# Two models in one kernel: x in eight chunks, the last weight rows loaded twice, and a new order of steps

## The chip, the cores and the metric

The kernel runs on one core of a Trainium2 chip. The metric is the device time of one execution in microseconds (us); less is better. TensorE (PE, with its weight loads PEld), VectorE (DVE), ScalarE (ACT), GpSimd (POOL) and SyncE (SP, which here only issues DMAs) each work through their own list of instructions strictly in order and wait for each other by semaphores.

## The reference, cut to what matters

Two independent models read a [2048, 448] input each and their outputs stand side by side in one [2048, 896] output. B, C and Lam are complex.

```
# A: 16 heads of 28, each token attends to 8 keys, 2 tokens apart
q, k, v = split(x_A @ wqkv)
logits[s, w] = q[s] . k[s - 2 w] * 28 ** -0.5        (w = 0..7, masked below token 0)
out_A = (softmax(logits) @ v[s - 2 w]) @ wo

# B: a diagonal state space model over the 2048 tokens
Bu = x_B @ (((Lam_bar - 1) / Lam) * B).T
h[t] = Lam_bar * h[t-1] + Bu[t]
out_B = 2 * real(h @ C.T) + x_B * Dskip
```

## The kernel before, in words

**Two tokens in one row.** x_A is read as [1024, 896]: a row holds an even token (columns 0 to 447) and the odd one behind it (448 to 895). For a product with the weights x has to stand with its columns on the partitions, so it is cut into chunks of 128 columns and each is transposed. With seven chunks (`xA`, [128, 7, 1024]) chunk 3 holds the even token's columns 384 to 447 on partitions 0 to 63 and the odd token's first 64 columns on partitions 64 to 127. The even token multiplies weight rows 0 to 447 as they come; the odd one needs the same rows shifted by 64 partitions. So `Wt` has seven chunks too, and six copies (`s1v`, `s2v`, `s1k`, `s2k`, `s1q` on DVE, `s2q` on ACT; lines 485 to 493) write the shifted weights on chip.

**The product.** `paired` (line 351) makes the steps of one product for 128 rows, which is 256 tokens: `e` are the three full matmuls of the even token, `o` those of the odd one, `f` both, `t` the two half-height matmuls on the last 64 weight rows. There are eight such products each of v, k and q (`v0` to `q7`, line 362 and 360 in the profile) and eight of the output projection (`w0` to `w7`). `ve`, `ke` and `qe` bring the sums from PSUM to SBUF; `kt` and `qt` then transpose the k and q rows by a transposed DMA into `Kt` and `Qt`. Four PSUM units are shared by number (the digit behind the engine letter in the list).

**How x gets there.** The first 512 rows (four tiles `xn`) come by plain loads and PE transposes them (`xt0a` to `xt3`, line 499, evacuated by `xe0a` to `xe3`). The last 512 rows come by transposed DMA straight from HBM: `xa2`, `xa3`, one DMA each (line 236). x_B comes by two transposed DMAs, `xb0` and `xb1`, of 512 rows each.

**Model B.** `nw` and `nt` load B into `natW` (`nt` are the four small loads of its last 64 rows), `lam0` to `lam6` mix them on DVE, `wtx0` to `wtx6` and `wr0` to `wr2` transpose the result by DMA into `WT`. `b30` to `b21` are the products with x_B (line 727; the second digit is the half of x_B, so `b11` is the first that reads what `xb1` brings), `ri`, `sc`, `ro` the scan on DVE. `ctn` and `ctl` load C and `c1m`, `c2m` mix it (line 540, with a first product `tc..` on POOL or ACT). `g0` to `g2` build a direct term. `y0` to `y7` are the output products (line 851 and 854); before a `y`, `xd` writes the skip term into PSUM from `xo`, which `xol` loads.

**Attention.** `s` are the logits of 128 rows, `x` the exponential on ACT, `a` the product with v, `n` the division on DVE, `ot` a transposed DMA, then the `w` products, `we` to SBUF and `wo` to HBM.

**The order.** Nothing is scheduled at run time. `ORDER` (line 27) is one list of steps, `name.engine` with the PSUM unit behind it, and each engine runs its steps in that order. All of SP's and ACT's DMAs run through eight semaphores, DMAHW0 to DMAHW7, handed out in turn: a DMA that takes a semaphore again is held on its issuing engine until the DMA that had it before has landed. POOL's DMAs have semaphores of their own (DMASW).

Of the kernel before, what the change touches and what calls it, by code (L numbers as in the profile page):

```python
# [32 lines left out]
lam1.V ve5.A0 q1t.P3 q1f.P3 tlam6.V qt0.S dia.G ve4.A1 td1.V k4f.P0 qe1.A3 xb0.S lam6.V k4t.P0 qe3.A2 td2.V v2t.P1
v6t.P3 tlam2.G v6f.P3 ke4.A0 p7.V v2o.P1 ve6.A3 v2e.P1 tlam4.G ts.A q6f.P2 wtx5.S q6t.P2 ctn.G k7t.P0 v7f.P3 ve2.V1
qe6.A2 wtx1.S v7t.P3 tb.V q5t.P2 ve7.A3 q5f.P2 kt3.S lam4.V tc.A cob.G b30.P1 qe5.V2 wtx0.S lam2.V s00.P be30.A1 qt1.S
k7f.P0 x00.A ri30.V wtx4.S b10.P1 sc300.V kt1.S ro30.V ke7.A0 ctl.S s01.P be10.A1 q4f.P0 x01.A ri10.V q4t.P0 k2t.P1
k2f.P1 qe4.A0 sc100.V s10.P qt2.S ke2.A1 b00.P0 sc101.V x10.A kt2.S ro10.V tc24.G kt7.S a00.P1 be00.A0 a01.P1 wtx6.S
s11.P tc23.G n0.V1 k5t.P0 x11.A k5f.P0 wtx2.S c24.V a10.P1 ri00.V tc21.G qt3.S ke5.A0 s20.P a11.P1 x20.A q7t.P0 xb1.S
q7f.P0 n1.V1 s21.P qe7.A0 c23.V k6f.P1 x21.A c21.V tc22.G k6t.P1 sc000.V a20.P0 qt4.S ke6.A1 s30.P sc001.V a21.P0
tc20.A kt6.S b20.P1 c22.V x30.A n2.V0 tc25.G kt4.S ro00.V kt5.S s31.P be20.A1 b11.P0 x31.A ot0.S c25.V ri20.V qt5.S  # L40
b31.P1 be11.A0 qt6.S c20.V sc200.V s40.P be31.A1 vg1.S b01.P0 tc12.A tc16.V qt7.S x40.A c16.V c12.V tc15.G ot1.S
sc201.V tc10.A s41.P be01.A0 c10.V a30.P1 a31.P1 c15.V tc14.A b21.P0 vg2.S n3.V1 x41.A tc11.G c14.V ot3.S kb.G c11.V
tc13.A s50.P ot2.S be21.A0 c13.V tc26.G a40.P1 ro20.V x50.A g1.P0 xol.G a41.P1 ge1.A0 s51.P ri11.V g0.P0 x51.A n4.V1
s80.P ge0.A0 c26.V ot4.S a50.P1 sc110.V x80.A a51.P1 wol.S g2.P0 n5.V1 gp2.A0 s60.P ge2.V0 x60.A a80.P1 ot5.S xd1.V0
n8.V1 y1.P0 sc111.V ot8.S xd0.V1 ro11.V s61.P y0.P1 x61.A ri21.V ye1.A0 yo1.S oc0.A a60.P0 sc210.V ye0.A1 yo0.S a61.P0
s70.P n6.V0 w3t.P1 x70.A w3f.P1 sc211.V ot6.S w0f.P0 we3.A1 wo3.S ro21.V w0t.P0 oc1.A s71.P we0.A0 wo0.S w4f.P1 x71.A
ri31.V w5f.P0 w5t.P0 w4t.P1 sc310.V w1t.P2 we4.A1 wo4.S w2t.P3 w1f.P2 we5.A0 wo5.S xd3.V1 w2f.P3 ro31.V we1.A2 wo1.S
# [930 lines left out]
```

## Time and profile before

| | us |
|---|---|
| time, median of 3 runs | 133.84 (133.19 to 134.24) |
| time of the profiled execution | 133.44 |
| span of its trace | 131.6 |
| PE busy | 123.5 (94% of the span) |
| DVE busy | 107.3 |
| ACT busy | 86.6 |
| POOL busy | 47.8 |
| granted PE clock | 0.995 |

The span is the stretch of the trace from the first to the last instruction; the time of the same execution is 1.84 us more. A row of the timeline gives start, duration, engine, line, operation and tiles. Rows with SPq, ACTq and POOL DMA are the issuing of a DMA and not the transfer; how long after the start of its issue a DMA has landed is listed apart. A row in the list of waits says who waited for whom: us in total, number of times, longest.

### The profile page before, as it was taken

How to read it: one execution, taken by the hardware profiler on the slowest of the kernel's cores; microseconds unless marked ns; L12 is line 12 of the kernel's file. 1: busy time of each engine (PE TensorE's matmuls, PEld its weight loads, DVE VectorE, ACT ScalarE, POOL GpSimd, SP SyncE). 2: the span in 40 equal slices, each digit the busy share in tenths (PEclk: the TensorE clock that was granted, in tenths of full speed). 3: DMA queues.
4: the chain of work that ended last, by engine and by line, in shares of the span. 5: the costliest groups of instructions: out<-in, count | busy, mean ns of one | idle time of the engine just before them, and what ended most of it. 6: DMA issues, size and time to landing. Idle time of an engine off the chain costs nothing.

```text
span 131.6 us, 3129 instructions
## 1 busy us (share of the span) xinstructions
PE 123.5 (94%) x1221; PEld 63.2 (48%) x1226; DVE 107.3 (81%) x225; ACT 86.6 (66%) x91; POOL 47.8 (36%) x75
## 2 busy tenths in 40 slices
PE   7899999999999999999999998799999999999960
PEld 2554444443444466544454656545644654445540
DVE  2569999998898999999999999999999999860000
ACT  3249779887999879968698957608797523222230
POOL 7998911899700946660077840000000000000000
PEclk9999999999999999999999999999999999999998
DMA  4999969799899995898979949890452652422222
GB/s 106 371 318 211 230 118 183 124 271 165 174 103 186 216 158 86 175 188 200 199 142 156 221 97 256 198 189 9 140 144 70 229 124 70 139 70 72 70 82 70
DMA packets 54546, 20.83 MB, mean 158 GB/s; under 512 B 46782, under 2 KB 54160, under 8 KB 54528
## 3 DMA queue, kind: packets, MB, share of 16 engines
q1 hardware_dynamic: 53376, 18.70, 69.4%
q0 software_dynamic: 656, 1.50, 4.0%
q10 hardware_dynamic: 496, 0.40, 0.9%
q8 instruction: 11, 0.18, 0.6%
q14 instruction: 7, 0.06, 0.2%
HBM read 5.30 MB, written 3.86 MB: 70 GB/s over the span
## 4 chain that ended last, share of the span: by engine, by line
PE 57%; DVE 29%; issue 4%; DMA 3%; POOL 2%; ACT 1%; SPq 0%; DVEq 0%
PE U L362 14%; PE U L851 11%; PE early L362 8%; PE late L851 4%; DVE rs L755 4%; PE U L854 3%; PE U L727 3%; DVE O L692 3%; PE U L360 3%; DVE natW L540 3%; DMA Wt<-in_A_wqkv_dram 3%; DVE C L540 3%; POOL wtmp L534 2%; DVE ra L742 2%; DVE rb L743 2%
## 5 line engine op out<-in xcount | busy, mean ns | idle before, releaser
L671 ACT ACTIVATE P<-s 128x1920 bf16<-128x1920 f32 (+1 forms) x16 | 28.6, 1786 | 5.7 <-PE s L649 5.6
L727 PE MATMUL U<-xB,WT 128*128 128x512 bf16 x93 | 22.1, 379 | 0.3
L362 PE MATMUL U<-Wt,xA 128*128 128x448 bf16 x90 | 19.7, 353 | 1.0 <-DVE Wt L339 0.5
L362 PEld LDWEIGHTS <-xA 128*128 128x128 bf16 x144 | 12.9, 98 | 15.1 <-issue 4.2
L534 POOL TENSOR_SCALAR wtmp<-CT,p_pah 128x448 f32<-128x448 bf16 x6 | 13.7, 2279 | 12.4 <-DVE rv L745 6.8
L335 ACT CAST ys<-U 128x896 bf16<-128x896 f32 (+1 forms) x11 | 9.5, 871 | 12.0 <-PE U L851 9.2
L851 PEld LDWEIGHTS <-h 128*128 128x128 bf16 x105 | 10.0, 98 | 9.2 <-DVE U L841 0.2
L727 PEld LDWEIGHTS <-WT 128*128 128x128 bf16 x98 | 9.2, 97 | 10.6
L362 PE MATMUL early<-Wt,xA 128*128 128x448 bf16 x54 | 11.7, 354 | 0.0
L335 ACT CAST u<-U 128x1024 bf16<-128x1024 f32 (+1 forms) x8 | 7.2, 905 | 4.5 <-PE U L727 4.4
L692 DVE TENSOR_TENSOR O<-U,rcs 128x896 bf16<-128x896 f32 (+1 forms) x9 | 9.8, 1090 | 0.3
L851 PE MATMUL U<-natW,h 128*128 128x448 bf16 x42 | 9.0, 353 | 0.1
L755 DVE TENSOR_TENSOR_SCAN rs<-p_r,ini,rv 128x512 bf16<-128x512 f32 x7 | 8.8, 1274 | 0.0
L680 PE MATMUL U<-Vt,P 128*128 128x29 bf16 x256 | 8.2, 176 | 0.6 <-DVE O L692 0.6
L755 DVE TENSOR_TENSOR_SCAN rs<-p_r,rv 128x512 bf16<-128x512 f32 x7 | 8.6, 1257 | 0.0
L680 PEld LDWEIGHTS <-P 128*128 128x128 bf16 x256 | 7.6, 96 | 2.1 <-issue 0.8
L335 ACT CAST ys<-late 128x896 bf16<-128x896 f32 (+2 forms) x6 | 4.3, 718 | 6.1 <-PE late L851 5.6
L362 PE MATMUL U<-wo,OT 128*128 128x448 bf16 x36 | 7.6, 353 | 0.0
L851 PE MATMUL U<-C,h 128*128 128x448 bf16 x35 | 7.4, 352 | 0.0
L335 ACT CAST Nx<-U 128x896 bf16<-128x896 f32 x7 | 6.4, 908 | 1.5 <-PE U L360 1.4
L534 POOL TENSOR_SCALAR wtmp<-CT,p_pag 128x448 f32<-128x448 bf16 x2 | 4.2, 2080 | 8.4 <-DVE C L540 8.4
L362 PEld LDWEIGHTS <-OT 128*128 128x128 bf16 x48 | 4.4, 98 | 4.9 <-issue 1.2
(198 smaller groups left out, 231.4 us busy)
## 6 DMA issues: line engine op xcount, KB each, us to landing
out_dram<-ys SPq DMA_DIRECT2D x15, 224.0 KB, 2.4
tmpB<-in_A_x_dram SPq DMA_DIRECT2D x4, 224.0 KB, 3.4
xo<-in_B_x_dram POOLq DMA_DIRECT2D x1, 896.0 KB, 8.0
Wt<-in_A_wqkv_dram SPq DMA_DIRECT2D x1, 672.0 KB, 5.8
wo<-in_A_wo_dram SPq DMA_DIRECT2D x2, 336.0 KB, 4.8
natW<-in_B_B_re_dram SPq DMA_DIRECT2D x1, 336.0 KB, 5.9
natW<-in_B_B_im_dram SPq DMA_DIRECT2D x1, 336.0 KB, 7.4
Wt<-in_A_wqkv_dram ACTq DMA_DIRECT2D x1, 224.0 KB, 3.5
```

What stands on the lines that cost most here:

```text
L335: ACT.copy(o, i)
L360: PE.matmul(ps(u_)[j], x()[r, 3, c], w()[r, 3], start=first, stop=not first, skip_group_check=True)
L362: PE.matmul(ps(u_)[j], x()[:, 4 * j + k, c], w()[:, 4 * j + k], start=(k == 0 and first), stop=(k == 2 and not first), skip_group_check=True)
L534: (G if e == "G" else V).tensor_scalar(view(held_t[name][:]), src(), scale(), None, ALU.mult)
L540: V.scalar_tensor_tensor(view(dst()), src(), scale(), view(t[:]), ALU.mult, ALU.add)
L671: ACT.activation(pv[:, :, :, c0:128], s4[:, :, 0:4 * n].rearrange("p g (s q) -> p g s q", s=4), ACTF.Exp, scale=SCALE)
L680: PE.matmul(U[u_][:, q, 29 * hd:29 * hd + 29], P[:, hd // 4, hd % 4, :], Vt[:, b, q, hd, :], start=(hd == 0), stop=(hd == H - 1), skip_gro ...
L692: V.tensor_tensor(O[0:n, :].rearrange("p (t h d) -> p t h d", t=2, h=H), av[0:n, :, :, 0:DH], rc.unsqueeze(3).to_broadcast((n, 2, H, DH)), ...
L727: PE.matmul(U[u_][:, j, :], WT[:, i, 128 * m:128 * m + 128], xB[:, i, HALF * hf:HALF * hf + HALF], start=(i == 0), stop=(i == 6))
L755: V.tensor_tensor_scan(rs[0][:, i], p["r2"][:, k:k + 1].to_broadcast((128, HALF)), rv[0][:, i], 0.0 if hf == 0 else ini[:, m:m + 1], ALU.m ...
L851: PE.matmul(ps[:, 0:D], hb[:, m, lo:lo + 128], C1()[:, m, :] if par else natW[:, m, 0:D], start=(m == 0 and par == 0), stop=(m == 6 and pa ...
L854: PE.matmul(ps[:, 0:D], xB[:, k, tk], Gm[:, k, :], start=False, stop=(k == 3), skip_group_check=True)
```

## The change

It does five things; apart from the order nothing else moves.

- x_A is cut into eight chunks that start at columns 0, 128, 256, 384, 448, 576, 704 and 768. The odd token now starts at a chunk border of its own, and its last 64 columns stand on partitions 64 to 127 of chunk 7. So even and odd token use the same three full weight chunks, the shifted copies are gone, and `Wt` has four chunks. PE transposes eight chunks for each of the four tiles and not seven.
- The last 64 weight rows are loaded twice, to partitions 0 to 63 and 64 to 127: two DMAs on ACT for v, two on SP for k and q, where there was one each.
- `xa2` becomes three transposed DMAs and `xa3` two.
- Buffers: 7 for q rows (5 before), 3 `wtmp` (2), 6 output rows `ys` (10). The results `w5` and `w6` go out in two DMAs each.
- A new list. `nt` moves from POOL to ACT, `ctn` from POOL to SP, `wol` (the load of wo) from SP to POOL, the last two evacuations from ACT to DVE, and about twenty other steps change engine. Six long and three short warm-up matmuls (`spin`, `sps`) stand ahead as before; five `sps` further on are gone and one `spin` is new.

```diff
-spin spin spin spin spin spin sps sps sps xt0a.P xt0b.P xe0a.A co0.G s1v.V xe0b.A sps sps v0e.P0 nw.S s2v.V nt.G sps
...
+spin spin spin spin spin spin sps sps sps xt0a.P xt0b.P xe0a.V co0.G v0e.P0 xe0b.V nw.S spin v0t.P0 con.G xt1.P xt2.P
+xe1.A xt3.P xe2.V v0o.P0 xe3.A v2o.P1 ve0.V0 v2e.P1 nt.A ctn.S k1f.P2 tr.P3 k1t.P2 p1.V3 k0t.P0 v2t.P1 ke1.A2 k0f.P0
...
-    xA = t_([128, 7, NP], BF16, "xA", "rA")
+    xA = t_([128, 8, NP], BF16, "xA", "rA")
-    Wt = t_([128, 7, 3 * D], BF16, "Wt", "rW")
+    Wt = t_([128, 4, 3 * D], BF16, "Wt", "rW")
-    Ns = [t_([128, 2, 512], BF16, f"N{i}")[:] for i in range(5)]
+    Ns = [t_([128, 2, 512], BF16, f"N{i}")[:] for i in range(7)]
...
+    CHUNK = (0, 128, 256, 384, D, D + 128, D + 256, D + 320)
...
-    ACT.dma_start(Wt[0:64, 3, VC], A_wqkv[384:448, VC])
+    for i in range(2):
+        ACT.dma_start(Wt[64 * i:64 * i + 64, 3, VC], A_wqkv[384:448, VC])
...
-    SP.dma_start(Wt[0:64, 3, KQ], A_wqkv[384:448, KQ])
+    for i in range(2):
+        SP.dma_start(Wt[64 * i:64 * i + 64, 3, KQ], A_wqkv[384:448, KQ])
...
-                    PE.matmul(ps(u_)[j], x()[r, 3, c], w()[r, 3], start=first, stop=not first, skip_group_check=True)
+                    PE.matmul(ps(u_)[j], x()[r, tail2 if j else 3, c], w()[r, 3], start=first, stop=not first, skip_group_check=True)
...
-                    PE.matmul(ps(u_)[j], x()[:, 4 * j + k, c], w()[:, 4 * j + k], start=(k == 0 and first), stop=(k == 2 and not first), skip_group_check=True)
+                    PE.matmul(ps(u_)[j], x()[:, 4 * j + k, c], w()[:, odd * j + k], start=(k == 0 and first), stop=(k == 2 and not first), skip_group_check=True)
...
-    for n in range(1, 4):
-        step[f"xa{n}"] = lambda e, u_, n=n: xbar_x(xA, xA2, n, 256)
+    for n in range(2, 4):
+        def f(e, u_, n=n):
+            tk = slice(256 * n, 256 * n + 256)
+            SP.dma_start_transpose(xA[:, 0:4, tk], xA2[tk, 0:512])
+            SP.dma_start_transpose(xA[:, 4:7, tk], xA2[tk, D:D + 384])
+            if n == 2:
+                SP.dma_start_transpose(xA[:, 7, 512:NP], xA2[512:NP, 2 * D - 128:2 * D])
+        step[f"xa{n}"] = f
...
-    free_y = list(range(10))
+    free_y = list(range(6))
...
-                Q[e].dma_start(outv[tk, :, lo:lo + D], lazy["ys"][:, i])
+                for pars in (slice(0, 1), slice(1, 2)) if (n, t) in HALVED else (slice(0, 2),):
+                    Q[e].dma_start(outv[tk, pars, lo:lo + D], lazy["ys"][:, i, pars])
```

Three places of the order matter for what follows. The first is ACT's list from its start, before. `xA` rows are the evacuations of transposed x, `Vt` and `Nx` those of v and k rows, `Wt<-Wt` is a shifted copy; in brackets stand the semaphores an instruction is held by.

```order
L243 DMA Wt<-in_A_wqkv_dram 128x2x448
L245 DMA Wt<-in_A_wqkv_dram 64x448
L335 ACT_TABLE_LOAD
L335 COPY xA<-x_143 128x3x128 [waits PE_49]
L335 COPY xA<-x_144 128x4x128 [waits PE_49]
L335 COPY xA<-x_143 128x7x128 [waits PE_49]
L335 CAST Vt<-U_93 128x32x28 [waits PE_49]
L335 COPY Wt<-Wt 64x4x448 [waits DMAHW7_49,DMAHW0_49]
```

The same place on ACT in the changed kernel; the four DMAs to `natW` and `Gm` are `nt`, the row behind them is `ke1`.

```order
L339 ACT_TABLE_LOAD
L339 COPY xA<-x_152 128x8x128 [waits PE_49]
L339 COPY xA<-x_151 128x8x128 [waits DVE_49,PE_49]
L519 DMA natW<-in_B_B_re_dram 64x448 [waits DMAHW2_49]
L520 DMA natW<-in_B_B_im_dram 64x448 [waits DMAHW3_49]
L521 DMA Gm<-in_B_B_im_dram 64x448 [waits DMAHW4_49]
L522 DMA Gm<-in_B_B_re_dram 64x448 [waits DMAHW5_49]
L339 CAST Nx<-early_260 128x32x28 [waits DVE_49,PE_49,Activation_49]
L402 ACTIVATE p_dt<-p_f_277 128x4 [waits DVE_49]
```

Four DMAs that POOL issued now stand in ACT's list ahead of the first k evacuation, each with a semaphore to wait for.

The second place is SP's list from the load of the k and q weights on, before. `Kt<-Nx` is the first `kt`.

```order
L248 DMA Wt<-in_A_wqkv_dram 128x3x896
L249 DMA Wt<-in_A_wqkv_dram 64x896 [waits DMAHW0_49]
L516 DMA natW<-in_B_B_re_dram 128x3x448 [waits DMAHW1_49]
L517 DMA natW<-in_B_B_im_dram 128x3x448 [waits DMAHW2_49]
L566 DMA_TRANSPOSE WT<-in_B_B_im_dram 128x3x64 [waits DMAHW3_49]
L236 DMA_TRANSPOSE xA<-in_A_x_dram 128x7x256 [waits DMAHW4_49]
L236 DMA_TRANSPOSE xA<-in_A_x_dram 128x7x256 [waits DMAHW5_49]
L566 DMA_TRANSPOSE WT<-in_B_B_im_dram 128x3x384 [waits DMAHW6_49]
L614 DMA_TRANSPOSE Kt<-Nx 128x8x128 [waits DMAHW7_49,DVE_49,Activation_49]
```

The same place in the changed kernel.

```order
L251 DMA Wt<-in_A_wqkv_dram 128x3x896 [waits DMAHW0_49]
L253 DMA Wt<-in_A_wqkv_dram 64x896 [waits DMAHW1_49]
L253 DMA Wt<-in_A_wqkv_dram 64x896 [waits DMAHW2_49]
L514 DMA natW<-in_B_B_re_dram 128x3x448 [waits DMAHW3_49]
L515 DMA natW<-in_B_B_im_dram 128x3x448 [waits DMAHW4_49]
L312 DMA Ctn<-in_B_C_re_dram 112x4x64 [waits DMAHW5_49]
L312 DMA Ctn<-in_B_C_im_dram 112x4x64 [waits DMAHW6_49]
L312 DMA Ctn<-in_B_C_im_dram 112x4x64 [waits DMAHW7_49]
L312 DMA Ctn<-in_B_C_re_dram 112x4x64 [waits DMAHW0_49]
L564 DMA_TRANSPOSE WT<-in_B_B_im_dram 128x3x64 [waits DMAHW1_49]
L618 DMA_TRANSPOSE Kt<-Nx 128x8x128 [waits DMAHW6_49,Activation_49]
L569 DMA_TRANSPOSE xA<-in_A_x_dram 128x4x256 [waits DMAHW7_49]
```

The load of the k and q weights now has a semaphore to wait for, four `ctn` loads stand behind `natW`, and the transposed loads of x stand behind the first `kt`, which waits for ACT.

The third place is SP's list ahead of `xb1`, before (`WT<-natW` are `wtx` steps).

```order
L614 DMA_TRANSPOSE Kt<-Nx 128x8x128 [waits DMAHW7_49,Activation_49]
L614 DMA_TRANSPOSE Kt<-Nx 128x8x128 [waits DMAHW0_49]
L550 DMA_TRANSPOSE WT<-natW 128x4x128 [waits DMAHW1_49]
L550 DMA_TRANSPOSE WT<-natW 128x4x128 [waits DMAHW2_49,DVE_49]
L614 DMA_TRANSPOSE Qt<-N_72 128x8x128 [waits DMAHW3_49]
L236 DMA_TRANSPOSE xB<-in_B_x_dram 128x7x512 [waits DMAHW4_49]
```

And in the changed kernel.

```order
L618 DMA_TRANSPOSE Kt<-Nx 128x8x128 [waits DMAHW5_49]
L548 DMA_TRANSPOSE WT<-natW 128x4x128 [waits DMAHW6_49]
L618 DMA_TRANSPOSE Qt<-N_74 128x8x128 [waits DMAHW7_49]
L548 DMA_TRANSPOSE WT<-natW 128x4x128 [waits DMAHW0_49,DVE_49]
L618 DMA_TRANSPOSE Qt<-N_72 128x8x128 [waits DMAHW1_49]
L236 DMA_TRANSPOSE xB<-in_B_x_dram 128x7x512 [waits DMAHW2_49]
```

From the first `kt` on, SP issues 21 transposed DMAs ahead of `xb1` before and 28 after: one more `qt`, the five pieces of `xa2` and `xa3`, and `wr1`; `kt4` stands there in place of `kt7`.

More of the change, by code (lines that the diff above doesn't have):

```diff
@@ L33 @@
[L33 to L47, printed above, removed]
@@ L51 @@
+ya7.P0 ye5.V1 yo5.S yb0.P3 ye7.A0 yp7.A yb1.P2 yf0.V3 yf1.V2 yq7.S
 """
@@ L524, in _ @@
         Q[e].dma_start(Pt[64:128, :], B_B_re[384:448, :])
-    tmps = [t_([128, D], F32, f"wtmp{i}") for i in range(2)]
+    tmps = [t_([128, D], F32, f"wtmp{i}") for i in range(3)]
     held_t = {}
```

50 lines of the change are left out of this document (29 added, 21 removed).

## The prediction, made before the changed kernel ran

> **What bounds the kernel now.** I read the page first.
>
> ```profile
> span 131.6 us, 3129 instructions
> PE 123.5 (94%) x1221; PEld 63.2 (48%) x1226; DVE 107.3 (81%) x225; ACT 86.6 (66%) x91; POOL 47.8 (36%) x75
> ...
> DMA  4999969799899995898979949890452652422222
> ```
>
> PE is busy for 94% of the span. A change can only move the time by moving PE's idle time or its work. To see where PE idles I cut the trace into stretches (columns: stretch, length, then busy time of PE, PEld, DVE, ACT, POOL with instruction counts, clock, DMA share, GB/s) and asked who PE waits for (us in total, times, longest).
>
> ```profile
> 3.00:6.00 3.00, 2.69 (x25) 1.70 (x24) 1.16 (x1) 1.13 (x3) 2.99 (x6) 1.00 1.06 370
> ...
> 78.00:81.00 3.00, 2.38 (x67) 1.71 (x66) 2.93 (x7) 1.92 (x3) 0.00 (x0) 1.00 0.80 297
> 81.00:84.00 3.00, 2.20 (x59) 1.49 (x56) 2.96 (x4) 2.24 (x3) 0.00 (x0) 1.00 1.02 95
> 84.00:87.00 3.00, 2.86 (x35) 1.72 (x32) 2.75 (x6) 0.65 (x1) 0.00 (x0) 1.00 1.66 315
> ```
>
> ```profile
> PE U L682 <- DVE O L692: 0.8, 1, 0.8
> PE U L680 <- DVE O L692: 0.6, 1, 0.6
> ```
>
> PE's idle time is small: 0.31 us in the stretch from 3 to 6 and 0.47 ahead of 6.78 (next part), and 0.62 + 0.80 + 0.14 = 1.56 us between 78 and 87 us, where it waits for divisions on DVE. From `y1` on (84.77 us, below) PE does not stop until its end. So what counts is when `y1` starts, and each us there is a us of the time.
>
> **The front.** Removed are five copies on DVE and one on ACT.
>
> ```profile
> 3.71 0.69 PE L499 MATMUL x<-eye,tmpB 128*128 128x128 bf16 x7
> ...
> 4.84 1.88 DVE L339 COPY Wt<-Wt 64x1344 bf16<-64x1344 bf16 x2 [3.09 <-DMA Wt<-in_A_wqkv_dram]
> ...
> 6.78 0.73 PE L362 MATMUL U<-Wt,xA 128*128 128x448 bf16 x3 [0.47 <-DVE Wt L339]
> ...
> 9.05 1.37 DVE L339 COPY Wt<-Wt 64x1344 bf16<-64x1344 bf16 x2
> 10.12 1.68 ACT L335 COPY Wt<-Wt 64x1792 bf16<-64x1792 bf16 x1
> 11.52 0.67 DVE L339 COPY Wt<-Wt 64x1344 bf16<-64x1344 bf16 x1
> ```
>
> DVE gets 1.88 + 1.37 + 0.67 = 3.9 us back and ACT 1.68. PE's 0.47 us wait goes, and most of the filler around it. By 6.78 us PE has done 14 transposes and three matmuls. What such work costs back to back stands in the chain of waits (start, us, what):
>
> ```profile
> 7.50 0.78 PE x L499 x14
> 8.28 0.57 PE U L362 x3
> ```
>
> So 0.78 + 0.57 = 1.35 us of work took the 3.07 us since the first transpose at 3.71: about 1.7 us lost. In the new list PE loses before `v0e` what the first evacuation takes, some 0.5 us as before, then a `spin` (0.2 to 0.4) and perhaps 0.2 until the second tail load is there: 0.9 to 1.1, an estimate. Four more transposes cost 4 x 0.056 = 0.22. I take 0.5 us gained by the first k product, with the sign open if the k and q weights are late (next). The wider copies to `xA` (1024 for 896 columns, a seventh of 0.6 to 0.9 us each) lie beside PE's transposes.
>
> **The loads, and ACT's wait.** These rows are the issuing on SP, on ACT, and the times from issue to landing (KB each, median us).
>
> ```profile
> 1.32 0.53 ACTq L245 DMA_DIRECT2D Wt<-in_A_wqkv_dram  x1
> 3.15 0.43 SPq L248 DMA_DIRECT2D Wt<-in_A_wqkv_dram  x1
> 4.34 0.60 SPq L249 DMA_DIRECT2D Wt<-in_A_wqkv_dram  x1
> 4.98 0.58 SPq L516 DMA_DIRECT2D natW<-in_B_B_re_dram  x1
> 5.60 0.49 SPq L517 DMA_DIRECT2D natW<-in_B_B_im_dram  x1
> ...
> 18.05 1.23 SPq L614 DMA_TRANSPOSE Kt<-Nx  x1
> 19.33 1.40 SPq L566 DMA_TRANSPOSE WT<-in_B_B_re_dram  x1
> ...
> 38.26 1.45 SPq L574 DMA_TRANSPOSE CT<-in_B_C_re_dram  x1
> 39.75 1.58 SPq L575 DMA_TRANSPOSE CT<-in_B_C_im_dram  x1
> 41.50 1.22 SPq L576 DMA_TRANSPOSE CT<-Ctn  x1
> ...
> 51.98 4.19 SPq L236 DMA_TRANSPOSE xB<-in_B_x_dram  x1
> ```
>
> ```profile
> SPq L249 <- DMA Wt<-in_A_wqkv_dram: 0.7, 1, 0.7
> ...
> Wt<-in_A_wqkv_dram SPq DMA_DIRECT2D x1, 672.0 KB, 5.8
> natW<-in_B_B_im_dram SPq DMA_DIRECT2D x1, 336.0 KB, 7.4
> Ctn<-in_B_C_re_dram POOLq DMA_DIRECT2D x2, 56.0 KB, 3.6
> xB<-in_B_x_dram SPq DMA_TRANSPOSE x2, 7.4
> ```
>
> The wait row shows the rule of the eight semaphores: before, SP's ninth DMA stood 0.7 us until ACT's first had landed, at 4.34. One DMA more ahead of it makes the large k and q load the ninth, so it is issued at 4.34 instead of 3.15. It landed at 3.15 + 5.8 = 8.95; it now lands between that (it stood behind the x tiles anyway) and 10.1. PE asks for it near 9: 0 to 1 us, which the 0.5 above just covers.
>
> Each `nt` DMA on ACT takes the semaphore of the DMA eight before it, so the last three wait for both `natW` loads and for the first `ctn` to land, and ACT stands in front of `ke1` until then. SP issues that `ctn` at 4.34 + 0.43 + 2 x 0.60 + 0.58 + 0.49 and five gaps of 0.05, at 7.3. Alone it would land 3.6 later, at 10.9. But `natW`, in front of it, landed at 5.60 + 7.4 = 13.0 before and is issued 1.1 later: 14.1. The DMA row of the page is at 9 all through this stretch, so I take the middle of the two, 12.5. Then comes the last issue (0.53, as L245), `ke1` (0.91, a row of ACT's evacuations) and gaps: `ke1` ends at 14.0 (12.4 to 15.6). PE needs its PSUM unit for `q1t` at about 13.6 (from 9.1 on three `f` of 1.14, and nine half-height or smaller steps of about 0.12), and what `ve2` and `ke0`, 0.9 each, free behind it 0.3 and 0.5 later. `ke0` ends near 15.8, so PE loses some 1.5 us here.
>
> ```profile
> 12.94 0.91 ACT L335 CAST Nx<-U 128x896 bf16<-128x896 f32 x1
> ```
>
> **SP's queue.** `kt1` waits for `ke1`, and behind `kt1` stands everything else that SP transposes. Before, the first `kt` went out at 18.05 and SP issued nearly without a break until `xb1` at 51.98. These are its issues by line (ns minimum/median/maximum).
>
> ```profile
> L614 SPq DMA_TRANSPOSE Kt<-Nx x8: 1232/1310/2255, 18.1 to 61.2; - x8
> L550 SPq DMA_TRANSPOSE WT<-natW x7: 1189/1264/2298, 20.9 to 48.3; - x7
> L566 SPq DMA_TRANSPOSE WT<-in_B_B_im_dram x2: 1287/1610/1932, 6.1 to 14.1; - x2
> L236 SPq DMA_TRANSPOSE xA<-in_A_x_dram x2: 1998/3275/4552, 7.5 to 12.1; - x2
> ```
>
> From `kt1` to `xb1` the new list has 28 of them: ten `kt`/`qt` at 1.31 (13.1), seven `wtx` at 1.264 (8.85), `wr1` at 1.93, five pieces of x at 1.24 (6.2), and and, as in SP's timeline above, `wr0` at 1.40, `xb0` at 4.19 like `xb1`, and `ctl` at 1.45 + 1.58 + 1.22, together 9.84. Sum 39.9, with 28 gaps of 0.05 41.3. The pieces of x have no row: the smallest transposed DMAs of the trace, with 4 to 8 blocks of 128 x 128, all take 1.2 us, so a piece is no cheaper than that. Below, five pieces could cost the 4.0 us of the two whole ones at their fastest; above, 9.1 at their slowest. The same sum for before's 21 (nine, seven, and the 9.84) gives 31.5, and the trace has 33.9, so the method is not too dear.
>
> [...]
>
> So `xb1` goes out at 14.0 + 41.3 = 55.3 and lands at 55.3 + 7.4 = 62.7. Before, it landed at 51.98 + 7.4 = 59.4, and PE used it at 59.85:
>
> ```profile
> 59.85 4.71 PE L727 MATMUL U<-xB,WT 128*128 128x512 bf16 x20
> ...
> 84.77 1.50 PE L851 MATMUL U<-natW,h 128*128 128x448 bf16 x7
> ```
>
> `b11` is the first to read it in both lists, and the steps ahead of it on PE are the same set. PE, 0.5 ahead and 1.5 lost at `ke1`, would be there at about 60.9 and waits 1.8 us. So `b11` starts at 62.7, 2.85 later than before. What is behind it up to `y1` is again the same set but for idle time: DVE has 3 us more to do its divisions, so the 1.56 us that PE lost there go. `y1` is then 2.85 - 1.56 = 1.3 us later.
>
> **What I cost at nothing.** `xol` now waits for `b31`, the last product to read `WT`, some 9 us ahead of `y1`, and took 8.0 us to land before; it is late by as much as `b31`. `wol` goes to POOL behind it and is needed by `w3` about 9 us after `y1`; its cover is two `y` products of 3.4 us, and if it lands later PE waits there for the difference. Six output buffers serve results that come every 1.7 us or more and leave within 2.4 us. Two more DMAs for `w5` and `w6` fall where SP waits for ACT. The last two evacuations on DVE cost about what ACT took (0.66 together). Buffers for q rows and `wtmp` only take waits away. The sum is one number: +1.3 us on 133.44 is 134.7, and 135.1 against the median, since the profiled execution is 0.4 under it.
>
> **The rivals.**
>
> 1. *SP keeps up.* ACT's wait is short because the small `ctn` load does not stay behind `natW` (lands at 10.9, `ke1` ends at 12.4), and the five pieces cost 4.0. Then `xb1` goes out at 12.4 + 39.1 = 51.5, no later than before, `b11` does not wait, the 0.5 of the front stays and the 1.56 of DVE waits go: 133.84 - 2.1 = 131.8. It decides at `ke1`: every us earlier there is a us earlier at `b11`. For it speaks that DVE has 3.9 us of slack; against it the DMA row at 9.
> 2. *No difference.* `ctn` lands at 11.5 and SP's pace is as summed: `xb1` lands at 61.7, `b11` is 1.85 late and the DVE waits pay for 1.56 of that: 133.84 + 0.3 = 134.1, give or take 0.3.
> 3. [...] The pieces of x issue at the slowest of the two loads before (9.1 instead of 6.2): `xb1` is 2.9 later again, 138.0. Against it: by then `natW` has landed.
>
> **How the numbers follow.** The forecast gets 0.50 (134.4 to 136.6, which is `ke1` from 13.3 to 15.5), rival 1 0.21, rival 2 0.17, rival 3 0.12. One per cent, 1.34 us, is about what a measurement of this kernel can tell from no change. Slower by more than that, above 135.2: the upper 0.30 of the forecast's case, since the late end of ACT's wait is the likelier one, and rival 3: 0.42. Within it: the other 0.20 and rival 2: 0.37. Faster: rival 1, 0.21. The range from 131.9 to 137.2 leaves out half of rival 1 and nearly all of rival 3.
>
> **What would show it.** ACT stands for 2 us or more in front of the first k evacuation, released by a DMA; the first `kt` goes out near 14.0; `xb1` is issued at 55 to 56 and PE waits for it at `b11` for 2 us or more; no PE wait for DVE between 78 and 87. If `xb1` goes out before 53 the forecast is wrong, and if PE reaches `b11` after `xb1` has landed, the loss, if any, is in another place.

## The result, and the profile after

| | before | after |
|---|---|---|
| median of the runs shown together | 133.81 us (133.19 to 134.24, 4 runs) | 141.86 us (140.12 to 143.83, 4 runs) |
| the profiled execution | 133.44 us, span 131.6 | 140.35 us, span 138.5 |
| `y1` starts | 84.77 us | 90.82 us |

The changed kernel is slower, by a ratio of 1.049 (95% interval 1.045 to 1.054). The forecast was 135.1 us with a range to 137.2: the direction held and the size did not. Repeats of the new kernels fall into two groups some 3 us apart, and of these two the ratios compare only the undisturbed group; medians are given over all repeats.

The page's head for the changed kernel, with the row of the clock that TensorE was granted:

```profile
span 138.5 us, 3132 instructions
PE 126.4 (91%) x1226; PEld 63.7 (46%) x1226; DVE 104.9 (76%) x225; ACT 83.4 (60%) x86; POOL 42.3 (31%) x72
...
PEclk9999999999999999995999999999999999999997
```

Before's row of the clock:

```profile
PEclk9999999999999999999999999999999999999998
```

PE's share has fallen from 94% to 91%. One slice in the middle of the clock row reads 5, where before's row has 9 up to its last slice, which lies behind PE's end in both kernels. What PE waited for (us in total, times, longest):

```profile
PE s L653 <- DMA Qt<-N: 1.7, 1, 1.7
PE U L731 <- DMA xB<-in_B_x_dram: 1.0, 1, 1.0
...
PE U L365 <- DMA Wt<-in_A_wqkv_dram: 0.6, 1, 0.6
PE early L367 <- DMA Wt<-in_A_wqkv_dram: 0.6, 1, 0.6
PE U L365 <- ACT Vt L339: 0.5, 1, 0.5
PE U L365 <- ACT Nx L339: 0.4, 1, 0.4
PE early L365 <- ACT Nx L339: 0.3, 1, 0.3
```

The waits for DVE that before had at 78 to 87 us are gone. In their place stand waits for DMAs, and three for ACT's evacuations of v and k rows. ACT's own timeline shows where these three come from (start, us, what, idle before):

```profile
11.22 0.47 ACTq L519 DMA_DIRECT2D natW<-in_B_B_re_dram  x1
11.98 0.49 ACTq L520 DMA_DIRECT2D natW<-in_B_B_im_dram  x1
13.30 0.47 ACTq L521 DMA_DIRECT2D Gm<-in_B_B_im_dram  x1
13.81 0.61 ACTq L522 DMA_DIRECT2D Gm<-in_B_B_re_dram  x1
14.54 0.91 ACT L339 CAST Nx<-early 128x896 bf16<-128x896 f32 x1 [5.31 <-DMA natW<-in_B_B_im_dram]
```

The four `nt` loads go out one by one as earlier loads land, and `ke1` starts 5.31 us after ACT's last work, released by a DMA. It ends at 15.45. SP's timeline has what follows from it; the last three rows are `xb0`, `qt3` and `xb1`:

```profile
15.47 1.23 SPq L618 DMA_TRANSPOSE Kt<-Nx  x1
16.75 2.44 SPq L569 DMA_TRANSPOSE xA<-in_A_x_dram  x1
...
30.17 3.87 SPq L236 DMA_TRANSPOSE xB<-in_B_x_dram  x1
...
56.87 1.32 SPq L618 DMA_TRANSPOSE Qt<-N  x1
58.23 4.74 SPq L236 DMA_TRANSPOSE xB<-in_B_x_dram  x1
```

The same three in the kernel before (`xb1` went out at 51.98):

```profile
23.49 4.44 SPq L236 DMA_TRANSPOSE xB<-in_B_x_dram  x1
...
50.63 1.31 SPq L614 DMA_TRANSPOSE Qt<-N  x1
```

`kt1` is issued at the end of `ke1`, and `xb1` 42.8 us behind it. All three go out 6.2 to 6.7 us later than before. PE meets this queue earlier than at `b11`: at `b30`, at `s30`, and then in a way that no term of the prediction has (`b20` is the third row, `b11` the fourth, `y1` the last):

```profile
36.81 1.67 PE L731 MATMUL U<-xB,WT 128*128 128x512 bf16 x7 [0.99 <-DMA xB<-in_B_x_dram]
...
62.05 0.59 PE L653 MATMUL s<-Qt,Kt 28*128 28x120 bf16 x16 [1.71 <-DMA Qt<-N]
62.56 4.48 PE L731 MATMUL U<-xB,WT 128*128 128x512 bf16 x14
...
67.50 3.19 PE L731 MATMUL U<-xB,WT 128*128 128x512 bf16 x14
...
90.82 1.50 PE L855 MATMUL U<-natW,h 128*128 128x448 bf16 x7
```

The same fourteen matmuls take 4.48 us in `b20` and 3.19 in `b11`. The stretches of one us tell why (the figure behind POOL's count is the clock):

```profile
61.00:62.00 1.00, 0.00 (x0) 0.00 (x0) 1.00 (x2) 0.00 (x0) 0.33 (x1) 0.89 0.54 52
62.00:63.00 1.00, 0.95 (x18) 0.49 (x18) 0.97 (x2) 0.26 (x1) 0.00 (x0) 0.50 1.27 290
...
64.00:65.00 1.00, 1.00 (x4) 0.30 (x2) 0.93 (x4) 0.51 (x1) 0.00 (x0) 0.50 1.28 286
65.00:66.00 1.00, 1.00 (x5) 0.45 (x4) 0.07 (x1) 0.00 (x0) 0.00 (x0) 0.90 1.05 214
```

PE stood still for the whole us from 61, the clock fell to 0.50 at 61.8, and it was back at 65.2, 3.4 us later. So PE reached `b11` at 67.50, 7.65 us later than before (59.85), and by then `xb1` had landed: the last update of the semaphore that `b11` waits for stands at 65.20 in the trace (before at 59.80, with `b11` starting 0.05 us behind it), so PE came 2.3 us after it.

The sum: `y1` is 6.05 us later. PE's stops up to `y1` are 6.2 us from 3 us on against before's 3.0, which is 3.2 more. The slow clock costs 4.48 - 3.19 = 1.3. Of the other 1.5 us, some 0.8 can be put down to what a stop costs beside its idle time, an estimate: a matmul of 448 columns lasts 0.35 us and the next starts after 0.19 (twelve take 2.44), so each stop hides another 0.16, and there are five more of them. Four more transposes make 0.2, and 0.5 us is not accounted for.

### The profile page after: what moved, and what is told of

Read it like the earlier page. It is cut to its first block, busy times and chain, and to the rows that moved or that the text cites. A ratio compares the mean times of both kernels' runs of the same rounds, so it can differ in the third digit from the quotient of the medians.

```text
span 138.5 us, 3132 instructions
## 1 busy us (share of the span) xinstructions
PE 126.4 (91%) x1226; PEld 63.7 (46%) x1226; DVE 104.9 (76%) x225; ACT 83.4 (60%) x86; POOL 42.3 (31%) x72
## 4 chain that ended last, share of the span: by engine, by line
PE 47%; DVE 27%; DMA 17%; issue 3%; SPq 2%; ACT 1%
PE U L731 12%; PE U L855 11%; DMA xB<-in_B_x_dram 5%; DMA natW<-in_B_B_re_dram 4%; DVE rs L759 4%; DMA Qt<-N 4%; PE U L367 4%; PE late L367 3%; PE U L858 3%; PE U L684 3%; DVE natW L538 3%; PE U L786 3%; DMA Wt<-in_A_wqkv_dram 3%; DVE O L696 2%; PE late L855 2%
## 5 line engine op out<-in xcount | busy, mean ns | idle before, releaser
L731 PE MATMUL U<-xB,WT 128*128 128x512 bf16 x98 | 23.8, 396 | 1.0 <-DMA xB<-in_B_x_dram 1.0
L367 PEld LDWEIGHTS <-xA 128*128 128x128 bf16 x144 | 12.9, 98 | 15.6 <-issue 3.4
L339 ACT CAST ys<-U 128x896 bf16<-128x896 f32 (+1 forms) x9 | 7.7, 864 | 14.3 <-PE U L855 8.3
L532 POOL TENSOR_SCALAR wtmp<-CT,p_pah 128x448 f32<-128x448 bf16 x5 | 8.4, 1686 | 17.4 <-DMA CT<-in_B_C_im_dram 15.2
L367 PE MATMUL early<-Wt,xA 128*128 128x448 bf16 x48 | 10.2, 353 | 0.6 <-DMA Wt<-in_A_wqkv_dram 0.6
L855 PE MATMUL U<-natW,h 128*128 128x448 bf16 x49 | 10.4, 353 | 0.2 <-DVE U L845 0.2
L532 POOL TENSOR_SCALAR wtmp<-CT,p_pag 128x448 f32<-128x448 bf16 x3 | 5.4, 1819 | 14.1 <-DVE C L538 11.8
L855 PE MATMUL U<-C,h 128*128 128x448 bf16 x42 | 8.9, 353 | 0.0
L653 PE MATMUL s<-Qt,Kt 28*128 28x120 bf16 (+1 forms) x256 | 6.4, 216 | 1.7 <-DMA Qt<-N 1.7
L339 ACT CAST ys<-late 128x896 bf16<-128x896 f32 x5 | 4.5, 906 | 5.0 <-PE late L365 4.7
L365 PE MATMUL U<-Wt,xA 64*128 64x448 bf16 x32 | 5.4, 355 | 1.6 <-DMA Wt<-in_A_wqkv_dram 0.6
L653 PEld LDWEIGHTS <-Kt 28*128 28x128 bf16 x256 | 5.1, 94 | 3.7 <-issue 2.0
```

The lines of the kernel that those rows point to most:

```text
L339: ACT.copy(o, i)
L365: PE.matmul(ps(u_)[j], x()[r, tail2 if j else 3, c], w()[r, 3], start=first, stop=not first, skip_group_check=True)
L367: PE.matmul(ps(u_)[j], x()[:, 4 * j + k, c], w()[:, odd * j + k], start=(k == 0 and first), stop=(k == 2 and not first), skip_group_check= ...
L532: (G if e == "G" else V).tensor_scalar(view(held_t[name][:]), src(), scale(), None, ALU.mult)
L653: PE.matmul(s4[:, g, s * n:s * n + n], Kt[32 * g:32 * g + DH, par, s, tk], Qt[32 * g:32 * g + DH, par, s, 128 * b + c0:128 * b + 128], sta ...
L731: PE.matmul(U[u_][:, j, :], WT[:, i, 128 * m:128 * m + 128], xB[:, i, HALF * hf:HALF * hf + HALF], start=(i == 0), stop=(i == 6))
```

## The experiments

The theory when they began: ACT's wait holds `ke1`, `ke1` holds `kt1`, and SP issues its transposes one after the other from there, so everything moves with `kt1`. The rivals: SP's pace and the pieces of x; the layout itself; the clock.

**Run 1: `nt` back on POOL.**

```
-... v2e.P1 nt.A ctn.S k1f.P2 ...
+... v0t.P0 nt.G con.G xt1.P ...
```

> The changed kernel with the four nt loads issued by POOL again, ahead of con, so that ACT has no wait for natW in front of ke1. Theory A (ACT's wait holds ke1, ke1 holds kt1, and SP issues from there on almost without a break, so everything behind moves with kt1): ke1 ends near 12.4 instead of 15.45, kt1 goes out 2 to 3 us earlier than 15.47, qt3 is there before s30, the PE waits of 1.3 us at 15 to 18 us and of 1.7 us at s30 and the slow matmuls behind it go: 135 to 137 us. Rival B (SP's own pace, with more and dearer pieces, is what is late): kt1 goes out earlier, but SP stands idle or slower later, qt3 and xb1 come out within 1 us of before, 139 to 141 us. Rival C (nt on POOL is late for its users, or POOL's queue pays): a new wait for nt or con, over 141 us.

Measured: 141.29 us (140.33 to 141.92), ratio 1.057 (1.050 to 1.065): nothing won. ACT's wait is gone, and yet `kt1` goes out only 0.33 us earlier. SP's timeline, with `wr2` in the third row and `kt1` in the fourth, and below it PE's first k product:

```profile
8.23 2.38 SPq L312 DMA_DIRECT2D Ctn<-in_B_C_im_dram  x2
11.34 2.10 SPq L312 DMA_DIRECT2D Ctn<-in_B_C_re_dram  x1
13.48 1.52 SPq L564 DMA_TRANSPOSE WT<-in_B_B_im_dram  x1
15.14 2.06 SPq L618 DMA_TRANSPOSE Kt<-Nx  x1
```

```profile
11.45 1.29 PE L367 MATMUL early<-Wt,xA 128*128 128x448 bf16 x6 [1.84 <-DMA Wt<-in_A_wqkv_dram]
```

Two other things hold `kt1` as late as ACT did. SP itself stands in the `ctn` loads, and `wr2` in front of `kt1` ends at 15.0. And the k and q weights land at 11.4, so that `ke1` ends at 14.2 without any wait of ACT for a load. The theory as stated fell: ACT's wait is one of three bounds that lie within 1.5 us of each other. From `kt1` to `xb1` it is 44.0 us, so SP's chain is no shorter than the changed kernel's 42.8.

**Run 2: the layout alone,** with before's list less its six copies.

```
-ORDER = the changed kernel's
+ORDER = before's, without s1v s2v s1k s2q s2k s1q
```

> The changed kernel's layout of x and weights, its loads and its buffers, with the list of before (less its six copies). Theory A (the loss is made by the list, through ACT's wait and kt1): within 1.5 us of the kernel before, 132.5 to 135 us; the copies' 0.5 us at the front are gained and the two or three dearer pieces of x on SP lose about 2 us, of which DVE's idle time pays part. Rival B (the layout itself costs: the five pieces of x on SP and the second tail load): 137 us or more, with xb1 or a qt waited for by PE.

Measured: 136.82 us (135.24 to 140.78), ratio 1.023 (1.014 to 1.033); the profiled execution took 135.24. The five pieces of x took 3.10 + 2.47 + 1.26 + 1.98 + 1.28 = 10.1 us of SP where before's two loads took 6.59, and the first `kt` goes out at 21.13 instead of 18.05. So the layout costs 2.3% by the ratio, with an interval from 1.4 to 3.3%. That the new list costs the rest of the 4.9% is a subtraction and was not run by itself. Theory A's band (to 135.0) was just missed by the profiled execution and clearly by the median: the first pieces are dearer than I had them. Later pieces take 1.3 us; that it is the plain loads beside them that make the early ones dear is likely, but was not tried.

**Run 3: PE kept busy ahead of `s30`.**

```
+                for i in range(10 if (b, par) == (3, 0) else 0):
+                    PE.matmul(s4[:, i % 4, :], ones[:, 0:128], ones, ...)
```

> The changed kernel with ten more matmuls of 128 x 512 into the score unit directly ahead of s30's own matmuls, so that PE is busy while it waits for qt3; they need no qt3 and their result is overwritten. Theory A (the 2 us stop of PE is what makes the clock fall to 0.50 for about 3 us behind it): b20 takes 3.1 to 3.3 us instead of 4.48, no window below 0.9, and the time falls by 1.0 to 1.4 us, to about 139.2 us. Rival B (the clock falls for another reason, such as the load of the chip at that place): b20 stays near 4.5 us and the time stays within 0.4 us of the changed kernel or grows by what of the ten matmuls sticks out.

Measured: 141.23 us (140.59 to 149.15), ratio 1.056 (1.048 to 1.063). In its profile the clock stays at 1.00 from 56 to 89 us and `b20` is back to full speed:

```profile
60.59 2.35 PE L649 MATMUL s<-const-bfloat16-1.0 128*128 128x512 bf16 x10
62.86 0.38 PE L651 MATMUL s<-msk 32*128 32x480 bf16 x4
63.08 0.38 PE L655 MATMUL s<-Qt,Kt 28*128 28x120 bf16 x16
63.39 3.19 PE L733 MATMUL U<-xB,WT 128*128 128x512 bf16 x14
```

`qt3` was issued 0.74 us later there than in the changed kernel (57.61), and `b11` still starts 0.46 us earlier, at 67.04. So the duration of `b20` is as theory A has it; the time is not, and the run does not show what the clock cost in the end. Its profiled execution was the one of 149 us: the load of `xo` took 13 us, PE stood 6.9 us in front of `y1`, and the clock was at 0.50 from 92.5 to 102.7.

**Run 4: before with `nt` on ACT,** one part alone.

```
-... v0e.P0 nw.S s2v.V nt.G sps ...
+... v1t.P1 nt.A ve0.A0 v3t.P2 ...
```

> The kernel before with one part of the change: the four nt loads go from POOL to ACT, in front of ve0. Theory A (a DMA on ACT takes the completion semaphore of the eighth DMA before it, so ACT stands until natW has landed near 13 us, whatever the rest of the list is): ACT waits 2 to 5 us ahead of the evacuation behind nt, released by a natW load; v, k evacuations are late, PE loses 2 to 4 us between 9 and 18 us; its DVE waits of 1.6 us at 78 to 87 pay for a part: 134.5 to 137 us. Rival B (the wait only arises with the extra load on SP and the ctn loads behind it): ACT waits under 1 us, the time is within 0.7 us of the kernel before.

Measured: 135.60 us (135.24 to 137.52), ratio 1.015 (1.010 to 1.020), as theory A said. ACT, and PE behind it:

```profile
12.64 0.91 ACT L335 CAST Vt<-U 128x896 bf16<-128x896 f32 x1 [3.69 <-DMA natW<-in_B_B_im_dram]
```

```profile
13.60 1.29 PE L362 MATMUL U<-Wt,xA 128*128 128x448 bf16 x6 [2.02 <-ACT Vt L335]
```

So the wait is real and costs 2 us by itself where nothing else is as late. The profiled execution, the one of 137.52 us, also had the clock at 0.50 from 14.9 to 18.3, behind this stop.

**Run 5: the changed kernel with `ctn` back on POOL; run 6: with both `nt` and `ctn` back.**

Run 6 has `nt.G` ahead of `con.G` as well.

```
-... v2e.P1 nt.A ctn.S k1f.P2 ...
+... v5t.P0 ctn.G cob.G q4t.P1 ...
```

> The changed kernel with the four ctn loads issued by POOL again, ahead of cob. SP's first transposed DMA (wr2) is then not behind ctn, and the nt loads on ACT take the semaphores of the k and q load and a tail load instead of natW's and ctn's. Theory A2 (two things hold SP's chain of transposes: ke1 through ACT's wait, and SP's own stand in the ctn loads; taking away only the first, as the run without ACT's wait showed, moves kt1 by 0.3 us): ACT waits under 2 us, ke1 ends near 13, wr2 goes out near 7.5, kt1 near 13 instead of 15.47, and qt3 and xb1 2 to 3 us earlier: 137 to 139 us. Rival B (SP's pace, not its start): xb1 goes out within 1 us of 58.23, 140 to 141 us. Rival C (ctn on POOL is late for CT): a wait on POOL or DVE behind cob, over 141 us.

> The changed kernel with both nt and ctn issued by POOL, as in the kernel before. Theory A2: no wait of ACT for a load, wr2 near 7.5, kt1 near 13, xb1 near 55.5; 137 to 139 us, like the run with ctn alone moved. What the early nt loads take from the k and q weights (which PE waited for 1.8 us with nt on POOL and ctn on SP) may cost 0.5 to 1 us of it. Rival B (SP's pace, not its start): xb1 within 1 us of 58.23, 140 to 141 us.

Measured: 141.37 us (139.38 to 142.03) and 142.60 us (139.68 to 143.25), before 133.67 beside them; neither has a ratio. `wr2` goes out at 7.57 and 7.20 as expected, but `kt1` at 14.52 and 14.41, since PE waits 1.8 and 2.0 us for the k and q weights, and `xb1` at 58.75 and 59.34: the chain from `kt1` on is 44 to 45 us long. Theory A2 had the start right and the end wrong; rival B has `xb1` in run 5, and misses it by 0.1 us in run 6 (within 1 us of the changed kernel's 58.23). The slow clock appears again, in another place, behind a stop at `b30` (run 5):

```profile
37.31 3.03 PE L731 MATMUL U<-xB,WT 128*128 128x512 bf16 x7 [2.64 <-DMA xB<-in_B_x_dram]
```

Seven matmuls take 3.03 us there and 1.67 in the changed kernel, and the clock is at 0.50 from 36.7 to 40.1.

**Run 7: run 6, with `wr2` and the first pieces of x directly behind `natW`.**

```
-... k0f.P0 wr2.S p2.A ... k3t.P3 xa2.S q1t.P2 ...
+... xe0b.V nw.S wr2.S xa2.S spin v0t.P0 ...
```

> The changed kernel with nt and ctn on POOL, and wr2 and the first three pieces of x (xa2) issued by SP directly behind natW, ahead of the first kt, so that the chain of transposes starts near 7.5 us as in the kernel before. Theory A2 (SP issues transposes one after the other, so what counts is when the first goes out and how much it has to issue; the stretch from 8 to 13 us, in which SP would stand for ke1, is used): xb1 goes out near 52.5 to 54 instead of 58.23, PE's waits at s30 and b30 go, 135 to 136.5 us. Rival B (transposes that start beside the plain loads slow those and are slow themselves, so nothing is won): the pieces take 2 to 3 us each, the k and q weights are later than 11 us, 138 us or more.

Measured: 138.98 us (138.05 to 139.34), ratio 1.038 (1.033 to 1.043). The first pieces cost 3.18 + 2.30 + 1.26 us there, `kt1` waits for them until 15.99, but from `kt1` on there are 25 transposes ahead of `xb1` instead of 28, and `xb1` goes out at 56.50, 40.5 us behind `kt1`. The interval ends below the changed kernel's 1.045, so this is a gain, of about 1%. The time lies in rival B's band (138 or more), and the reasons are B's too, pieces of 2 to 3 us and the k and q weights at 11.7; only "nothing is won" does not hold. A wait that runs 5 and 6 have as well (1.4 to 1.5 us) stands out now, PE in front of `y1` and of the next y product:

```profile
88.50 1.49 PE L855 MATMUL U<-natW,h 128*128 128x448 bf16 x7 [1.03 <-DVE U L845]
...
94.08 1.11 PE L855 MATMUL U<-natW,h 128*128 128x448 bf16 x5 [1.49 <-DVE U L845]
```

L845 is the skip's product of `xo`, whose load went out at 78.62, behind `b31`.

**Run 8: run 2, with each late stretch of x in one transposed DMA** (chunks 4 to 6 of those tokens then hold other columns, so the right ones are left out).

```
-            SP.dma_start_transpose(xA[:, 0:4, tk], xA2[tk, 0:512])
-            SP.dma_start_transpose(xA[:, 4:7, tk], xA2[tk, D:D + 384])
+            SP.dma_start_transpose(xA[:, 0:7, tk], xA2[tk, 0:2 * D])
```

> The changed kernel's layout with the list of before, as in the second run, but each of the two late stretches of x read by one transposed DMA of 896 columns and not by two of 512 and 384 (chunks 4 to 6 of these tokens then hold other columns: this leaves the right columns out); the one piece for chunk 7 stays. Theory A (the pieces are what the layout costs: they took 10.1 us of SP against 6.6 for before's two loads, and everything behind moved by 2 to 3 us): SP's x loads take 7 to 8.5 us, xb1 goes out 1.5 to 3 us earlier than 54.09, and the time is 133.2 to 134.5. Rival B (the number of DMAs does not matter, the bytes do): the three take 9.5 to 10 us, time within 0.4 us of the second run's 135.2.

Measured: 135.58 us (135.32 to 136.51), ratio 1.014 (1.011 to 1.016). The three loads took 5.06 + 1.26 + 2.52 = 8.8 us, between the two theories, and the first `kt` went out at 20.50, 0.6 us earlier than in run 2. Yet `xb1` went out at 55.19, later than run 2's 54.09: what was won was lost again behind the first `kt`, for example in `xb0`, whose issue took 6.01 us for 4.70. The time is rival B's (within 0.4 us of 135.2). What the number of pieces costs is not settled by it.

**Run 9: run 7, and half of the v weights' tail on POOL,** so that the k and q weights are the eighth DMA of SP and ACT again.

```
-        ACT.dma_start(Wt[64 * i:64 * i + 64, 3, VC], A_wqkv[384:448, VC])
+        (G if i else ACT).dma_start(Wt[64 * i:64 * i + 64, 3, VC], A_wqkv[384:448, VC])
```

> The run with nt and ctn on POOL and the early pieces of x, and now the second half of the v weights' tail issued by POOL instead of ACT, so that the large k and q weight load is the eighth and not the ninth DMA of the two fast queues and does not wait for the first x tile. Theory A3 (the k and q weights, late by that wait and asked for earlier by the new list, are one of the three things that hold ke1): the load goes out near 3.3 instead of 4.2, PE's wait for it falls from 1.7 to 1.0 us or less; since SP then issues its chain 0.7 us earlier, qt3, xb1 and y1 come 0.5 to 1 us earlier: 137.3 to 138.4 us. Rival B (the DMA engines are full there, and the load lands near 11.3 whenever it is issued): PE's wait stays over 1.4 us, 138.5 to 139.2 us.

Measured: 136.74 us (135.02 to 137.43), ratio 1.015 (1.008 to 1.022), better than either band: the ratio falls from run 7's 1.038 to 1.015, some 2% from one load of 56 KB. SP's rows of the weights, of the first `kt` with the one behind it, and of `xb1`:

```profile
3.14 0.43 SPq L251 DMA_DIRECT2D Wt<-in_A_wqkv_dram  x1
...
14.53 3.48 SPq L618 DMA_TRANSPOSE Kt<-Nx  x2
...
53.90 5.74 SPq L236 DMA_TRANSPOSE xB<-in_B_x_dram  x1
```

PE does not wait for weights at all, `kt1` goes out 1.46 us earlier than in run 7 and `xb1` 2.6. `y1` starts at 86.90 with 1.17 us of wait for `xo`'s product. The profiled execution is the slowest of the four.

**Run 10: run 9 with `xo` early; run 11: the changed kernel with `xo` early.**

```
-            lazy["ys"] = t_([128, 6, 2, D], BF16, "ys", "rW")
+            lazy["ys"] = t_([128, 6, 2, D], BF16, "ys", "rT")
-        xo = lazy["xo"] = t_([128, 9, D], BF16, "xo", "rT")
+        xo = lazy["xo"] = t_([128, 9, D], BF16, "xo", "rW")
-... g2.P0 xol.G be31.A1 ...
+... qt5.S xol.G tc13.G ...
```

> The same as the run before this one, and xo (the skip's x and D rows) put into the memory that the qkv weights leave, loaded near 65 us and not behind b31 (the output buffers go where xo was). Theory A4 (y1 needs DVE's product of xo, and xo lands 8 to 9 us after b31, so a b31 that is late moves y1 as well, and DVE and PE stood 1 to 2.5 us for it in the runs whose b11 was earlier): no wait of PE for that product, y1 0.8 to 2 us earlier, 135.8 to 137.2 us. Rival B (what y1 waits for is DVE's own list, not the load): the wait stays over 0.8 us, time within 0.5 us of the run without it.

> The changed kernel with that early xo alone. Theory A4 with the profile of the changed kernel (PE waited only 0.2 us there for xo's product, and its load was in time by 0.3 us): within 0.7 us of the changed kernel, 139.4 to 140.8 us, but without the runs of 142 us and over if those are runs in which the load was slow. Rival B (xo sets the time of y1 in it): 138.5 us or less.

Measured: 138.57 us (137.49 to 140.86), ratio 1.036 (1.026 to 1.046), and 143.26 us (141.31 to 144.73) without a ratio: both worse than without it. POOL came to the load at 54.23 in run 10, 1.7 us after SP's `xb1` (52.57), not near 65, and PE's `b11` shows the price:

```profile
63.70 4.56 PE L731 MATMUL U<-xB,WT 128*128 128x512 bf16 x14 [4.22 <-DMA xB<-in_B_x_dram]
```

PE had `xb1` 11.1 us after its issue, where this load landed after 7.0 us in the changed kernel, 7.8 before and at most 8.5 in the runs that leave `xo` late, and then PE took 4.56 us for a product of 3.19, in an execution whose mean clock was 0.983. The wait in front of `y1` is gone as A4 said; it was paid for at `b11`. In run 11 the load went out 1.1 us behind `xb1`, which PE had 9.5 us after its issue, with 1.68 us of wait at `b11`. But in that execution `kt1` was already 1.26 us later than in the changed kernel, whose list is the same up to there, so its time alone does not show what the early `xo` costs.

**Run 12: before with `ctn` on SP,** one part alone.

```
-... q6t.P2 ctn.G k7t.P0 ...
+... v3f.P2 ctn.S wr2.S p1.V3 ...
```

> The kernel before with its four ctn loads issued by SP ahead of wr2 instead of by POOL: one part of the change alone, which puts the start of SP's chain of transposes behind plain loads and their semaphores. Theory A2 (the start of the chain counts): wr2 goes out near 10 instead of 6.13, the first kt 1.5 to 2.5 us later than 18.05 (it had 2.0 us of idle ahead of it), xb1 1.5 to 2.5 us later than 51.98; PE waits at b11 for it by 1 to 2 us, of which the 1.6 us of DVE waits behind it pay most: 133.6 to 135 us. Rival B (the transposes are faster when the plain loads are out of the way, which gives the start back): x's two loads take 4 us instead of 6.6, kt and xb1 within 0.7 us of before, no change in time.

Measured: 134.98 us (134.59 to 136.76), ratio 1.010 (1.007 to 1.013). SP's rows, `wr2` third and `kt0` last:

```profile
7.04 1.68 SPq L308 DMA_DIRECT2D Ctn<-in_B_C_im_dram  x2
8.76 2.49 SPq L308 DMA_DIRECT2D Ctn<-in_B_C_re_dram  x1
11.29 2.48 SPq L566 DMA_TRANSPOSE WT<-in_B_B_im_dram  x1
...
19.72 1.24 SPq L614 DMA_TRANSPOSE Kt<-Nx  x1
```

`wr2` is 5.2 us later, `kt0` 1.67, `xb1` 2.05, `b11` 1.88, `y1` 1.44, the time 1.3: theory A2's chain, step by step, in smaller steps than it had (`b11` waits 0.51 us, not 1 to 2). Part of rival B holds too: the two transposed loads of x behind `wr2` took 4.35 us for 6.59, and with them most of the 5.2 us came back by `kt0`.

**Run 13: the changed kernel with run 9's repair alone** (the same edit).

> The changed kernel with one repair alone: the second half of the v weights' tail goes out on POOL, so that the k and q weights are the eighth DMA of the fast queues and wait for nothing. Theory A (ACT's wait for natW and ctn holds ke1 wherever the weights land): the weights go out near 3.2 and PE does not wait for them, but ACT still stands until 13 to 14 us, kt1 goes out within 1 us of 15.47, and the time is 139 to 140.3 us. Rival D (the weights were what set the time): kt1 goes out before 14, 137 to 138.3 us.

Measured: 139.37 us (138.49 to 143.21), ratio 1.043 (1.039 to 1.048), whose interval overlaps the changed kernel's. ACT still stands 4.63 us for `natW`, `ke1` starts at 13.72 and `kt1` goes out at 14.65, 0.8 us earlier: theory A, but for 0.30 us that PE still waits for the weights. The weights alone are not what set the changed kernel's time.

**Run 14: run 9 with `xo` loaded by SP behind `xb1`,** into the memory of run 10.

```
-... b01.P1 qt5.S tc13.G ...
-... g2.P0 xol.G be31.A1 ...
+... b01.P1 xol.S qt5.S tc13.G ...
```

> The run with all four repaired (nt and ctn on POOL, early pieces of x, weights as the eighth DMA), and xo in the memory of the qkv weights, loaded by SP behind the last k rows and qt7, so that it starts after the second load of x has landed and yet some 8 us ahead of b31. Theory A4 (y1 stood 1.2 and y0's follower 1.5 us for the product of xo): these waits go and the second load of x keeps its time, 134 to 135.6 us, 1 to 2 us under that run's median of 136.74. Rival B (DVE's list is late by itself, or the load takes from OT's transposes): within 0.6 us of that run, 136 to 137.4 us. A version that beats the kernel before would need 133.6 or less, which neither expects.

Measured: 136.95 us (134.54 to 137.28), ratio 1.015 (1.010 to 1.020), before 133.22. The wait in front of `y1` is gone and `xb1` keeps its time (the profile has no wait at `b11`), but the time is run 9's, within a spread of 2.7 us. In its profile PE stopped 1.41 us for `qt3` at `s30`, `b20` behind it took 4.54 us, where the other products of its size took 3.19, the mean clock was 0.98, and `y1` starts at 86.90, just as in run 9. Whether the load of `xo` costs anything in run 9 stays open. No version of the new list or layout beat the kernel before.

## Why the prediction was wrong, step by step

- **The front (+0.5 us gained): not seen.** PE asked for the k weights at 9.86, not near 9, and started at 10.42 after 0.56 us of wait. It also stood 0.61 us for the second tail load of v, forecast at 0.2.
- **The k and q load: right in place, too cheap.** It was issued at 4.33 (4.34 forecast). It landed at 10.3 in the profiled execution (8.95 to 10.1 given), and that was on the lucky side: with the same lists up to there PE got it at 11.1 and 12.0 in runs 3 and 11, after 1.4 and 2.2 us of wait. In runs 1, 5, 6 and 7, whose lists differ there, it got it at 11.4 to 11.8, after 1.7 to 2.0. It was costed at nothing net; runs 7 and 9 show that undoing it is worth 2 us once the other bounds are out of the way.
- **ACT's wait: right.** `ke1` ended at 15.45, at the upper end of 12.4 to 15.6; I took 14.0 because I had the first `ctn` load land at 12.5 and let that be the last thing to wait for. The profile names the second `natW` load, which landed at 13.3, and behind it two issues of 0.5 and 0.6 us follow each other without a wait. `ke1` itself moved by chance too: with the same front, `kt1` went out at 15.91 and 16.73 in runs 3 and 11. PE's loss there was 1.28 us of idle time in three stops (1.5 forecast). Run 4 shows the wait by itself. It was not the only holder of `kt1`, as the prediction had it: run 1.
- **SP's chain: right in kind and nearly in size.** 42.8 us from `kt1` to `xb1` for 41.3. The sum for before's own transposes had come out 2.4 us below the trace (31.5 for 33.9), and the prediction read that only as "not too dear": it was a sign that the sum is too cheap. So `xb1` went out at 58.23 (55.3) and was there at 65.2 (62.7).
- **"PE, 0.5 ahead and 1.5 lost at `ke1`, would be there at about 60.9": the step that failed.** The prediction followed one item of SP's queue, `xb1`, to its one reader, and let PE run free up to it. But the transposes ahead of it are late as well (`xb0` 6.7 us, `qt3` and `xb1` 6.2 against before), and each has a reader: PE stopped for `xb0` at `b30` (0.99), for `qt3` at `s30` (1.71) and, through the stop at `s30`, ran `b20` at half clock (1.3). It came to `b11` at 67.50, 6.6 us after the 60.9 of the forecast; 4.0 of these are the two stops and the slow clock, the rest is the front and smaller terms. It did not wait there: this is the case that the prediction names in its last sentence, a loss in another place. Had PE been free up to there, `b11` would have started at 65.2, and less the 1.56 us of DVE's waits `y1` would have been 3.8 us late: 137.6 us, an estimate, just past the end of the range. So of the 4.8 us by which `b11` came after the forecast's 62.7, 2.5 are `xb1` itself (`ke1` 1.45 late and the chain 1.5 longer, its landing 0.4 quicker) and 2.3 are PE's earlier stops and the clock, which the sum did not have.
- **The 1.56 us of DVE's waits go: right.** `b11` is 7.65 us late and `y1` 6.05, so 1.60 came back; run 12 gives back 0.44 of 1.88, as its DVE waits only shrink.
- **Costed at nothing: two were not.** `xo`, late with `b31`, was in time by a hair in the changed kernel (0.2 us of wait) and became a wait of 1.0 to 1.5 in runs 5, 6, 7, 9 and 13. And 0.5 us more lies behind PE's end (127.3 to 131.6 before, 133.6 to 138.5 after), nearly all of it behind the issue of the last DMA; this was not tried.
- **The rivals.** SP did not keep up. The pieces of x cost 7.6 us behind `kt1` (6.2 summed, 9.1 in the third rival) and 10.1 in run 2, where they lie beside the plain loads: the third rival's price is right for that place. The first rival had SP's issuing short, with `xb1` out at 51.5; SP's issue of 28 transposes is the 42.8 us that decide.

The three parts made one at a time in the kernel before cost 2.3% (layout, interval 1.4 to 3.3), 1.5% (`nt` on ACT) and 1.0% (`ctn` on SP). Their sum is near the whole 4.9%, but the sum is not an explanation: taken out of the changed kernel one at a time, `nt`, `ctn` and the weights bring at most some 0.6%, with intervals that overlap the changed kernel's or with no ratio at all, since each hides behind the others (runs 1, 5 and 13), and only all together, with the early pieces of x, bring it to 1.5% (run 9), which is inside the interval of what the layout cost in run 2. The other steps of the new list that change engine (27, counted from the two lists) were not tried apart.
